# Turning p with a VectorE block transpose, with V laid out to match, in a decode kernel of two layers

## The chip, the cores and the metric

The kernel runs on one core of one Trainium2 chip. The metric is device time of one execution in microseconds. Runs are marked fast or slow by their length (slow: over 1.5% above the fastest of the same kernel). Of a kernel's runs I compare the fast ones, and medians are quoted over all runs unless said otherwise. A ratio is the mean time of one kernel's fast runs over that of the other's of the same rounds, so it is not quite the ratio of the medians quoted.

## The reference

Four tokens go through attention and a gated feed-forward block, twice, with the same weights and caches:

```python
def _A_ref(x, k_cache, v_cache, wq, wo):      # x (4, 1, 448), caches (4, 8, 8192, 256)
    W = min(4096, max(256, Sk // 4))          # 2048 rows of each cache are used
    ...                                       # 16 query heads share 8 key/value heads
    scores = jnp.einsum("bhqd,bhkd->bhqk", q, k) * (Dh ** -0.5)
    p = _softmax(scores, axis=-1)
    o = jnp.einsum("bhqk,bhkd->bhqd", p, v)
    ...
x = x + _A_ref(_layernorm(x), ...)
x = x + _B_ref(_layernorm(x), ...)            # silu(x Wg) * (x Wu), then Wd
x = x + _A_ref(_layernorm(x), ...)            # the same once more
x = x + _B_ref(_layernorm(x), ...)
```

One K or V tile of a token and head is 2048 x 256 bf16, 1 MB. There are 32 of each per layer, 128 MB for two layers; what fits in on-chip memory is kept between the layers, and about 94 MB of caches and 12 MB of weights are loaded. The arithmetic is small. The kernel is a stream of loads with work hung on it.

## The kernel before

The program builds a graph of operations, schedules it on a model of the engines at build time, and emits one instruction stream per engine. All loads are issued by SyncE, in order, on one queue. Buffers (`half`, 27 of 512 KB) are handed out as they come free. These are the parts that matter, for a single head (a group); some groups join two heads.

```python
ksrc = A_k_cache[t, kvh, ...].rearrange("(p j) d -> p (j d)", p=128)
for hf, cell in enumerate(kc):                 # two transfers of 512 KB, 128 partitions each
    dma_start(half[cell][:, :], ksrc[:, 2048 * hf:2048 * hf + 2048])
    VectorE: transpose of 32x32 blocks, in place
vsrc = A_v_cache[t, kvh, ...].rearrange("(a q g) d -> q a g d", a=4, q=128)
for hv, cell in enumerate(vs):                 # two transfers of 512 KB, 128 partitions each
    dma_start(half[cell][:, :].rearrange("p (a g d) -> p a g d", a=2, g=4),
              vsrc[:, 2 * hv:2 * hv + 2, :, :])
...
# scores: 32 matmuls of 128 columns into 4 blocks of 32 partitions of a PSUM bank
# maximum (VectorE), spread over the head's rows (2 matmuls), negated (VectorE)
exp   (ScalarE): praw <- scores
turn  (PE):      4 matmuls with praw as the stationary operand -> PSUM
copy  (ScalarE): pT <- PSUM
total (PE):      row sums of p;   pv (PE): 16 matmuls  V^T pT -> Y
...
# normalise, collect, output projection
```

Filler matmuls on zeros (line 1098) are put into PE's gaps: 282 of them, 95 us, in the profile of before.

## Time and profile before

| | before |
|---|---|
| time, median of the first 3 runs | 312.2 us (310.85 to 312.75) |
| DMA engines busy | 92.9% of the span, 106.55 MB |
| PE, VectorE, GpSimd, ScalarE busy | 81%, 63%, 28%, 22% |
| first and last packet of loaded data | 2.1 us, 295.2 us of 313.2 |
| loads of V | 98 of 512 KB |
| loads of K | 82 of 512 KB |

The page's busy shares are averages over the whole span, so a stretch that starves is hidden in them. The useful question to the trace is: in which stretches are the DMA engines busy, and how many GB/s do they move then? Both kinds of loss are in the trace of before. At 264 to 272 us the share is 0.73, with 236 GB/s moved, and the queue's sequencer had waited for PE to be done with a buffer, up to 4.8 us at a time. At 10 to 14 us the share is 1.02 and yet only 238 GB/s are moved.

### The profile page before, as it was taken

The page shows a single profiled execution, that of the slowest core. Times are in us where ns is not written, and L with a number is a line of the kernel's source. Part 1 is how long each engine was busy: PE and PEld are TensorE (multiplying, and loading weights), DVE is VectorE, ACT ScalarE, POOL GpSimd, SP SyncE. Part 2 cuts the span into 40 slices and gives each one's busy share as a digit, 9 for nine tenths or more (in the row PEclk, how much of TensorE's full clock was granted, in tenths as well). Part 3 has the DMA queues.
Part 4 walks back from the last instruction along what each step waited for, and adds up shares of the span by engine and source line. Part 5 has one row for each costly group of instructions (what it writes and reads, how often), then busy time and mean ns, then how long its engine had stood idle before and what let it go on. Part 6 is the DMA issues. An engine that isn't in the chain of part 4 may idle for free.

```text
span 313.2 us, 11054 instructions
## 1 busy us (share of the span) xinstructions
PE 255.0 (81%) x4814; PEld 129.5 (41%) x4814; DVE 198.1 (63%) x627; ACT 68.1 (22%) x196; POOL 87.1 (28%) x236
## 2 busy tenths in 40 slices
PE   4788777869598867898988785988969779888996
PEld 1323323424123543264444252544435444445563
DVE  8527945845114995559778565699776656585532
ACT  0030010303003121143322032203403231423310
POOL 1521011303202322134342031441505133332530
PEclk9999999999959997799999997589999986999995
DMA  7999999999999999999999999779999998999500
GB/s 275 317 394 401 403 401 393 397 391 346 271 387 343 306 409 393 386 340 383 397 400 394 398 395 393 281 254 374 383 334 369 391 394 314 300 387 390 206 2 3
DMA packets 45024, 107.25 MB, mean 342 GB/s; under 512 B 3240, under 2 KB 8880, under 8 KB 44592
## 3 DMA queue, kind: packets, MB, share of 16 engines
q1 hardware_dynamic: 44976, 106.55, 92.9%
q8 instruction: 38, 0.62, 0.8%
q14 instruction: 10, 0.08, 0.1%
HBM read 106.53 MB, written 0.00 MB: 340 GB/s over the span
## 4 chain that ended last, share of the span: by engine, by line
PE 37%; DMA 26%; DVE 15%; SPq 14%; issue 4%; ACT 3%; POOL 1%; DVEq 0%; ACTq 0%
DMA half<-in_A_v_cache_dram 13%; DMA half<-in_A_k_cache_dram 9%; DVE half L853 7%; PE Y L973 7%; PE A L1098 7%; SPq L848 6%; SPq L527 6%; PE S L883 5%; DMA wu_sb<-in_B_w_up_dram 4%; SPq L861 3%; PE A L1026 2%; DVE oh L990 2%; PE Z L617 2%; PE Y L943 2%; PE Y L996 1%
## 5 line engine op out<-in xcount | busy, mean ns | idle before, releaser
L853 DVE STREAM_TRANSPOSE half<-half 128x1024 uint32<-128x1024 uint32 x82 | 100.3, 1230 | 3.3 <-DMA half<-in_A_k_cache_dram 3.0
L1098 PE MATMUL A<-identb,small 128*128 128x512 bf16 x249 | 83.1, 435 | 0.0
L986 POOL TENSOR_TENSOR small<-small 128x2 f32<-128x2 f32 (+1 forms) x55 | 41.3, 753 | 62.1 <-DVE small L964 59.6
L973 PE MATMUL Y<-half,pT 128*4 128x256 bf16 (+1 forms) x1024 | 46.4, 283 | 10.7 <-DMA half<-in_A_v_cache_dram 6.5
L900 POOL TENSOR_TENSOR qe<-qc,tiny 128x64 bf16<-128x64 bf16 x64 | 18.3, 293 | 83.0 <-PE S L883 61.6
L988 ACT ACTIVATE oh<-Y 128x256 bf16<-128x256 f32 x55 | 21.1, 384 | 83.0 <-PE Y L973 71.9
L990 DVE SCALAR_TENSOR_TENSOR oh<-oh,small,Y 128x256 bf16<-128x256 bf16 x55 | 25.9, 470 | 19.0 <-ACT oh L988 18.5
L883 PE MATMUL S<-half,qe 128*8 128x128 bf16 x1472 | 30.6, 222 | 7.7 <-issue 3.6
L1098 PEld LDWEIGHTS A<-identb,small 128*128 128x128 bf16 x249 | 22.8, 109 | 20.7 <-issue 12.0
L907 DVE TENSOR_REDUCE tiny<-S 104x1 bf16<-104x128 f32 (+1 forms) x55 | 16.8, 306 | 22.8 <-PE S L883 17.5
L883 PEld LDWEIGHTS S<-half,qe 128*8 128x8 bf16 x1472 | 21.8, 85 | 17.1 <-DVE half L853 5.9
L929 ACT ACTIVATE praw<-S,small 104x128 bf16<-104x128 f32 x46 | 16.8, 365 | 55.5 <-DVE small L921 54.7
L973 PEld LDWEIGHTS Y<-half,pT 128*4 128x4 bf16 (+1 forms) x1024 | 18.6, 83 | 21.4 <-DMA half<-in_A_v_cache_dram 11.7
L1026 PE MATMUL A<-wo_sb,oT 128*4 128x448 bf16 x208 | 17.8, 358 | 2.5 <-DVE oT L1006 2.1
L951 ACT ACTIVATE pT<-Y 128x64 bf16<-128x64 f32 (+1 forms) x55 | 13.2, 240 | 20.7 <-PE Y L943 17.6
L996 PE MATMUL Y<-tiny,oh 128*128 128x2 bf16 (+1 forms) x110 | 11.0, 170 | 5.9 <-DVE oh L990 5.1
L912 PE MATMUL S<-small,identb 104*104 104x32 bf16 x55 | 11.2, 214 | 5.7 <-DVE tiny L907 4.9
L580 POOL TENSOR_SCALAR st<-st 128x1 f32<-128x1 f32 x16 | 4.3, 266 | 41.4 <-DVE st L569 41.3
L921 DVE TENSOR_REDUCE small<-S 104x1 f32<-104x32 f32 x55 | 9.0, 177 | 9.4 <-PE S L915 9.2
L943 PE MATMUL Y<-sel,praw 104*128 104x32 bf16 x184 | 12.1, 180 | 2.0 <-ACT praw L929 2.0
L773 ACT ACTIVATE wide<-A 128x448 bf16<-128x448 f32 x14 | 7.6, 544 | 27.6 <-PE A L707 15.8
L895 PE MATMUL S<-half,qe 128*8 128x256 bf16 x288 | 9.9, 274 | 4.2 <-DVE half L853 3.0
(137 smaller groups left out, 296.5 us busy)
## 6 DMA issues: line engine op xcount, KB each, us to landing
half<-in_A_v_cache_dram SPq DMA_DIRECT2D x98, 512.0 KB, 8.9
half<-in_A_k_cache_dram SPq DMA_DIRECT2D x82, 512.0 KB, 8.3
wo_sb<-in_A_wo_dram SPq DMA_DIRECT2D x8, 448.0 KB, 13.3
wq_sb<-in_A_wq_dram SPq DMA_DIRECT2D x3, 1024.0 KB, 6.9
wd_sb<-in_B_w_down_dram SPq DMA_DIRECT2D x1, 1568.0 KB, 15.2
wg_sb<-in_B_w_gate_dram SPq DMA_DIRECT2D x2, 672.0 KB, 12.7
wu_sb<-in_B_w_up_dram SPq DMA_DIRECT2D x2, 672.0 KB, 13.0
wq_sb<-in_A_wq_dram SPq DMA_DIRECT2D x2, 256.0 KB, 11.4
```

The lines of the kernel that those rows point to most:

```text
L527: g.dma(rank, nbytes, lambda e: e.dma_start(dst, src), f"w{nw[0]}", w=key if isinstance(key, tuple) else (key,), run=run)
L848: g.dma((pp - KLEAD if pp <= LAST1 else pp + KTAIL) + OFF.get(("k", t, layer, kvh), 0), 1 << 19, lambda e, cell=cell, hf=hf, ksrc=ksrc: e. ...
L853: return e.transpose(a, a)
L883: last = e.matmul(Sb[s_][qd:qd + 8, 0:128], lhsT=qe[q_][:, 0, ce, :, :].rearrange("p a n -> p (a n)"), rhs=kt[:, ce // 2, ce % 2, 2 * x:2 ...
L900: g.op(POOL, 0.25, pos - SLEAD - 1, lambda e, P=P, t=t, kvh=kvh: e.tensor_tensor(qe[q_][:, P, :, :, :], qc[t][:, kvh, :, :].unsqueeze(2).b ...
L943: last = e.matmul(o, lhsT=praw[0:R, c0:c0 + 128], rhs=w, start=(gg == 0 and h == 0), stop=False, skip_group_check=True)
L973: last = e.matmul(Yb[p_][32 * gg:32 * gg + M, 256:512], lhsT=pT[pt][:, gg, 2 * hv + a, 4 * P:4 * P + M] if n == 2 else p1[:, gg % 2, gg // ...
L986: g.op(POOL, 0.69, pos, lambda e: e.tensor_tensor(ri[p_][:, 0:2 * n], rs[p_][:, 0:2 * n], expo[:, 1:1 + 2 * n], op=ALU.pow), r=(f"rs{p_}", ...
L988: g.op(SCA, 0.34, pos, lambda e: e.activation(oh[:, :], Yb[p_][:, 256:512], ACT.Copy), r=(f"y{p_}",), w=("oh",), bank=(f"Y{p_}",))
L990: g.op(DVE, 0.43, pos, lambda e: e.scalar_tensor_tensor(out=oh[:, :], in0=oh[:, :], scalar=lomask[:, 0:1], in1=Yb[p_][:, 256:512], op0=ALU ...
L1026: last = e.matmul(Ab[32 * k:32 * k + B, 0:D], lhsT=oT[oi][:, k % 2, k // 2, :], rhs=wo_sb[:, 4 * kvh + k, :], start=False, stop=False, ski ...
L1098: g.filler = lambda b: lambda e: e.matmul(fbank[b][:, 0:512], lhsT=zero[:, 0:1].broadcast_to([128, 128]), rhs=identb[:, :].unsqueeze(1).br ...
```

## The change

The intent is to turn p (rows of the head by position) into pT (position by rows) with one VectorE transpose of 32x32 blocks, SBUF to SBUF, in place of four PE matmuls and a ScalarE copy out of PSUM. In the kernel's index arithmetic each block stays on its own 32 partitions, so V's rows must lie on the partitions that the blocks dictate: the upper 64 partitions hold rows 1024 away from those of the lower 64. No single step from partition to partition gives these rows, and the kernel splits each V load in two.

```diff
-                    ksrc = A_k_cache[...].rearrange("(p j) d -> p (j d)", p=128)
+                    ksrc = A_k_cache[...].rearrange("(h p j) d -> h p (j d)", h=2, p=128)
...
-                    vsrc = A_v_cache[...].rearrange("(a q g) d -> q a g d", a=4, q=128)
+                    vsrc = A_v_cache[...].rearrange("(h b a s j) d -> h b s a (j d)", h=2, b=2, a=2, j=4)
...
-                        e.dma_start(half[cell[0]][:, :].rearrange("p (a g d) -> p a g d", a=2, g=4),
-                            vsrc[:, 2 * hv:2 * hv + 2, :, :])
+                        [e.dma_start(half[cell[0]][64 * h:64 * h + 64, :].rearrange("p (a x) -> p a x", a=2),
+                            vsrc[h, hv]) for h in range(2)]
...
-            g.op(PE, ..., turn, ...)
-            g.op(SCA, ..., lambda e: e.activation(pf, Yb[p_][:, 0:PW], ACT.Copy), ...)
+            g.op(DVE, 0.14, pos, lambda e: e.transpose(
+                pT[pt][...].bitcast(UINT32)..., praw[...].bitcast(UINT32)), ...)
```

Cut from it: groups of two heads are gone; the query is expanded twice per head; the norm does one power of three numbers on GpSimd in place of three operations; the last residual is written straight into the output layout, and the output copy is split over two engines; the filler has one density while loads remain and a higher one afterwards; and the plan of heads, the lead of each load and the set of tiles kept between the layers are all set anew.

## The prediction

The 1230 ns under "p's turn" and the 1.23 us of rival 2 are K's transpose in the trace of before (128x1024 uint32, 82 times). The queue's sequencer, which the prediction has waiting for PE, waited longest in sum for the matmuls on V (L973): 29.1 us in 13 waits.

> **What bounds the kernel now.** I read the page first: the busy shares, the slices, the DMA queues and the chain of waits.
>
> ```profile
> PE 255.0 (81%) x4814; PEld 129.5 (41%) x4814; DVE 198.1 (63%) x627; ACT 68.1 (22%) x196; POOL 87.1 (28%) x236
> ...
> q1 hardware_dynamic: 44976, 106.55, 92.9%
> ...
> PE 37%; DMA 26%; DVE 15%; SPq 14%; issue 4%; ACT 3%; POOL 1%; DVEq 0%; ACTq 0%
> ```
>
> The 16 DMA engines are busy 92.9% of 313.2 us; no compute engine but PE comes near. PE's 255 us contain 95 us of filler matmuls (the group of line 1098: 249 writing A, 83.1 us, and 33 writing Z, 12.0 us) [...], so PE is not the bound in amount. The chain names PE more often than DMA because a buffer comes free when PE has read it and the queue's sequencer waits for that. This is a loading kernel with a short start and a tail. I then asked for stretches of the span (start and end, length, busy time and count per engine, granted clock, DMA share, GB/s):
>
> ```profile
> 5.00:10.00 5.00, 1.79 (x5) 0.65 (x3) 4.39 (x38) 0.00 (x0) 0.00 (x0) 1.00 1.01 423
> 10.00:14.00 4.00, 3.85 (x14) 1.72 (x14) 1.53 (x13) 0.00 (x0) 2.96 (x9) 1.00 1.02 238
> 14.00:18.00 4.00, 3.75 (x27) 1.20 (x30) 0.76 (x5) 0.00 (x0) 2.65 (x8) 1.00 1.06 380
> 66.00:72.00 6.00, 3.73 (x45) 1.22 (x43) 3.13 (x6) 1.06 (x5) 0.70 (x1) 1.00 1.05 386
> 72.00:76.00 4.00, 3.63 (x84) 1.82 (x85) 2.18 (x9) 2.41 (x9) 1.48 (x3) 1.00 1.05 382
> 76.00:80.00 4.00, 3.14 (x49) 1.73 (x52) 1.69 (x12) 0.00 (x0) 1.76 (x5) 1.00 1.08 246
> 82.00:86.00 4.00, 1.56 (x17) 0.47 (x14) 0.69 (x1) 0.11 (x1) 0.00 (x0) 1.00 1.10 238
> ...
> 192.00:208.00 16.00, 15.26 (x246) 7.58 (x241) 12.16 (x42) 3.17 (x12) 6.40 (x18) 0.58 0.79 290
> 264.00:272.00 8.00, 7.17 (x174) 4.06 (x162) 4.96 (x16) 3.50 (x10) 2.01 (x4) 1.00 0.73 236
> 294.00:313.00 19.00, 15.47 (x325) 9.80 (x323) 6.03 (x32) 2.34 (x7) 5.29 (x12) 0.78 0.02 6
> ```
>
> Three kinds of loss show. First, at 192 to 208 and 264 to 272 the DMA share falls to 0.79 and 0.73: the queue starves, in the first case at a granted clock of 0.58. Second, from 294 on nothing is loaded: a tail of 19 us. Third, and decisive here, at 10 to 14, 76 to 80 and 82 to 86 the engines are fully busy (1.02, 1.08, 1.10) and yet move only 238 to 246 GB/s, against 380 to 423 on either side. The code says what lies there: 3 MB of query weights issued from 1.15 us and moved at 423 GB/s from about 2.3 us end at about 10 us, and next in the queue come their last 64 rows, sent as two transfers, one into partitions 0 to 63, one into 64 to 127. The other two stretches hold the last 64 rows of the gate and up weights, sent the same way.
>
> ```profile
> half<-in_A_v_cache_dram SPq DMA_DIRECT2D x98, 512.0 KB, 8.9
> half<-in_A_k_cache_dram SPq DMA_DIRECT2D x82, 512.0 KB, 8.3
> ...
> wq_sb<-in_A_wq_dram SPq DMA_DIRECT2D x2, 256.0 KB, 11.4
> ```
>
> V is 98 transfers of 512 KB (51.4 MB, nearly half of all bytes), each over all 128 partitions. The change turns each into a pair of 256 KB with the same shape of destination as the last line's.
>
> [...]
>
> **The change part by part.**
>
> *V's transfers.* The loss of one pair, read from the stretches: 10 to 14 us moved 238 x 4 = 952 KB, which at 400 GB/s (between the neighbours' 423 and 380) takes 2.4 us, so 1.6 us were lost. 76 to 80: 984 KB at 382 is 2.6 us, lost 1.4. 82 to 86: 952 KB at 386 is 2.5 us, lost 1.5. The first pair is of exactly V's new size, 2 x 256 KB, 1.36 us at 386 GB/s; with the loss about 2.9 us, some 180 GB/s, which is half rate or a little under. If every pair of V loses what half rate costs, 98 x 1.36 = 133 us. It is not hidden: the DMA engines are the bound, and a busy share near 1 leaves nothing to put it in. [...] I put an in-between case at half of it, 65 us (an estimate of mine, worked from the same 1.36 us).
>
> *Bytes.* Layer 0 keeps 22 K tiles instead of 23 and 15 V tiles as before, so K has 84 loads instead of 82: 1.05 MB more, 2.7 us at 386 GB/s, on the path.
>
> *Issues.* V goes from 98 to 196 issues. The shortest issue is about 0.37 us and a typical one 0.47, so a pair takes 0.9 us of the sequencer, under the 1.36 us of data: hidden, though a starved queue refills more slowly.
>
> *p's turn.* Removed per single group: 4 matmuls of 180 ns (12.1 us in all, pipelined, about 0.26 us a group in the timeline) and a ScalarE copy of 222 ns; 13.2 us of ScalarE in all with the paired groups. Added: 64 VectorE transposes of 128x64 uint32. 1230/1024 is 1.2 ns a column, so 0.08 us plus a start that I take from small VectorE instructions here (155 to 180 ns): about 0.2 us, 13 us in all. The chain of one group loses one hop and about 0.5 us; groups overlap, so this counts once or twice, in the tail.
>
> *No paired groups.* 46 single and 9 paired groups become 64 single ones. The nine more cost VectorE about 9 x (284 + 177 + 180 + 470) = 10 us, less the longer forms they replace (9 x 419 = 4 us for the maximum alone); with 2 more K transposes (2.5 us) VectorE goes from 198 to some 218 us. GpSimd gets a second query expansion per head, 64 x 293 ns = 18.8 us, and loses two of three small operations per norm, 16 x (266 + 298) = 9 us: about 100 us. Neither is a bound.
>
> *Tail.* The last update is one operation instead of five, the output copy (0.61 us) is split over two engines, fillers are denser once all loads are issued (the clock in 304 to 312 was 0.53). Together with p's turn I take 1.5 us, so 17.5 us of tail.
>
> *The new order.* Plan, lead times and filler density are all set anew, which may fill the starved stretches. What they cost now: V 51.4 MB at 386 is 133 us, the other 55.2 MB at an average of 380 (weights included) 145 us, start 2, tail 19: 299 us, against 313 measured, so about 14 us.
>
> The sum: V 133, the rest 56.2 MB at 380 = 148, start 2, tail 17.5: 300 us with neither loss. With V in pairs: 365 at half of the loss, 433 at all of it. With slower loading, starvation no longer adds, as buffers come free in time.
>
> **The rivals.** (1) *Pairs run at full rate in a long stream.* The three slow stretches are isolated pairs among full-width transfers; nothing in the trace shows fifty in a row. For it: the two halves are adjacent in the queue, and the 16 engines report one transfer done over a spread of about 2 us[...]. Whoever wrote the change also set everything anew around it, which one hardly does for something slow. Against it: these very pairs were adjacent too, and lost all the same. Then the time is 300 us plus what of the starvation stays, 302 to 314. (2) *VectorE or GpSimd becomes the bound*, because K's transpose (84 x 1.23 = 103 us) shares VectorE with the longer softmax chain: at some 218 us of work this costs single microseconds through late buffers. For it: VectorE has 15% of the chain. It would make 310 to 318 out of (1). (3) *Only the bytes and the tail count*, 2.7 against 1.5 us: 313, the same.
>
> **Range and chances.** I give the pairs' loss about two in three: a third to nearly all of it (410 to 433), a third to part of it (330 to 400), and a third to rival 1 with its variants. The middle of this is about 370 us; I name that, with a range of 302 to 432. The gap between 315 and 330 is unlikely, so the range is wide because there are two outcomes, not because each is vague. Faster by over 2% needs less than 306: full-rate pairs and most starvation gone, 0.20. Same, 306 to 318.4: 0.13. Slower: 0.67.
>
> **What would show it.** Right: in the stretches with V, a DMA share near 1 at 200 to 300 GB/s instead of 386, packets of 2 KB that take longer, V's two transfers landing much later, PE waiting for V in the group of line 973's successor, VectorE's share falling. Wrong: 380 to 400 GB/s in V's stretches; then the trace decides between the tail, the dips and VectorE. The p step is right if the new transpose takes 0.15 to 0.25 us and no ScalarE copy stands between exponent and sums. The prediction fails by its first step if the loss of a lone pair is not that of a stream.

## The result, and the profile after

The changed kernel took 422.89 us (median of 4 runs, 416.42 to 424.23), the kernel before 312.48 us (4 runs, 310.85 to 314.88). The ratio is 1.340, 95% interval 1.320 to 1.361: slower by a third. Two of the four runs are slow, the fast ones took 416.42 and 421.59 us. The profiled run is a fast one. Its page, busy shares, queue and chain:

```profile
PE 289.5 (70%) x4851; PEld 139.5 (34%) x4851; DVE 222.2 (54%) x747; ACT 75.5 (18%) x160; POOL 98.4 (24%) x254
...
q1 hardware_dynamic: 46832, 107.60, 97.8%
...
DMA 61%; PE 18%; SPq 14%; DVE 4%; issue 2%; ACT 0%; DVEq 0%
```

The DMA engines are busier than before (97.8% against 92.9%) with one megabyte more to move in 101 us more. The chain is now 61% DMA, where it was 26%. Every compute engine's share fell. The stretches of the changed kernel say how the loads went (start and end, length, busy time and count of PE, PE's loads, VectorE, ScalarE, GpSimd, then granted clock, DMA share, GB/s):

```profile
20.00:26.00 6.00, 4.46 (x93) 2.11 (x93) 6.00 (x13) 0.56 (x1) 2.13 (x8) 1.00 1.07 248
40.00:44.00 4.00, 0.93 (x10) 0.22 (x10) 1.32 (x2) 0.00 (x0) 0.00 (x0) 1.00 1.08 240
200.00:240.00 40.00, 28.07 (x534) 13.24 (x535) 23.83 (x76) 9.82 (x21) 11.58 (x32) 0.74 1.00 257
240.00:280.00 40.00, 30.70 (x543) 16.05 (x543) 28.12 (x85) 8.06 (x18) 10.24 (x27) 0.74 1.05 303
398.60:414.60 16.00, 13.44 (x287) 8.60 (x283) 6.11 (x29) 2.96 (x8) 2.24 (x3) 0.85 0.01 2
```

Rates near those of three short stretches before (238 to 246 GB/s at a full share) now hold for most of the span: 240 to 303 here. PE's granted clock is 0.74 in the long stretches; why is not shown. The tail is 16.0 us after the last loaded packet (at 398.6), against 18.0 before (from 295.2). The issues and the waits for V:

```profile
half<-in_A_v_cache_dram SPq DMA_DIRECT2D x196, 256.0 KB, 11.9
half<-in_A_k_cache_dram SPq DMA_DIRECT2D x84, 512.0 KB, 13.7
```

```profile
PEld Y L918 <- DMA half<-in_A_v_cache_dram: 61.9, 40, 6.5
PE Y L918 <- DMA half<-in_A_v_cache_dram: 57.2, 40, 6.4
...
DVE half L837 <- DMA half<-in_A_k_cache_dram: 50.8, 34, 8.0
```

The same three waits before:

```profile
PEld Y L973 <- DMA half<-in_A_v_cache_dram: 11.7, 17, 2.0
...
PE Y L973 <- DMA half<-in_A_v_cache_dram: 6.5, 12, 1.5
...
DVE half L853 <- DMA half<-in_A_k_cache_dram: 3.0, 5, 1.0
```

The lists of waits give total wait, number of waits and the longest, in us. K's loads have not been touched in shape, yet they land 13.7 us after their issue instead of 8.3, and VectorE waits 50.8 us for them where it waited 3.0. So the slow V transfers hold up what stands behind and beside them.

The p step itself, first the lines of before (exponent, copy), then those of after (exponent, transpose):

```profile
L929 ACT ACTIVATE praw<-S,small 104x128 bf16<-104x128 f32 x46 | 16.8, 365 | 55.5 <-DVE small L921 54.7
...
L951 ACT ACTIVATE pT<-Y 128x64 bf16<-128x64 f32 (+1 forms) x55 | 13.2, 240 | 20.7 <-PE Y L943 17.6
```

```profile
L897 ACT ACTIVATE praw<-S,small 112x128 bf16<-112x128 f32 x64 | 34.8, 544 | 59.8 <-DVE small L894 52.9
...
L901 DVE STREAM_TRANSPOSE pT<-praw 128x64 uint32<-128x64 uint32 x64 | 15.0, 235 | 24.4 <-PE Y L918 23.1
```

The transpose takes 235 ns and replaces a copy of 240 ns (222 for a single head) and the matmuls ahead of it. But the exponent became 179 ns longer (544 against 365): it now writes p in an order that suits the transpose. I had not foreseen this.

### The profile page after: what moved, and what is told of

It reads as the page before. It is cut to its first block, busy times and chain, and to the rows that moved or that the text cites. A ratio compares the mean times of both kernels' runs of the same rounds, so it can differ in the third digit from the quotient of the medians.

```text
span 414.6 us, 11341 instructions
## 1 busy us (share of the span) xinstructions
PE 289.5 (70%) x4851; PEld 139.5 (34%) x4851; DVE 222.2 (54%) x747; ACT 75.5 (18%) x160; POOL 98.4 (24%) x254
## 3 DMA queue, kind: packets, MB, share of 16 engines
q1 hardware_dynamic: 46832, 107.60, 97.8%
## 4 chain that ended last, share of the span: by engine, by line
DMA 61%; PE 18%; SPq 14%; DVE 4%; issue 2%; ACT 0%; DVEq 0%
DMA half<-in_A_v_cache_dram 39%; DMA half<-in_A_k_cache_dram 22%; SPq L846 5%; SPq L832 5%; PE Y L918 5%; PE S L867 3%; SPq L512 3%; DVE half L837 3%; PE A L1042 2%; PE A L970 1%; PE Z L1042 1%; PE A L688 1%; PE Z L707 1%; PE Y L940 1%; PE Y L907 1%
## 5 line engine op out<-in xcount | busy, mean ns | idle before, releaser
L837 DVE STREAM_TRANSPOSE half<-half 128x1024 uint32<-128x1024 uint32 x84 | 103.5, 1235 | 50.9 <-DMA half<-in_A_k_cache_dram 50.8
L918 PE MATMUL Y<-half,pT 128*4 128x256 bf16 x1024 | 61.2, 351 | 58.7 <-DMA half<-in_A_v_cache_dram 57.2
L930 POOL TENSOR_TENSOR small<-small 128x2 f32<-128x2 f32 x64 | 44.7, 700 | 106.5 <-DVE small L911 101.8
L867 PE MATMUL S<-half,qe 128*16 128x128 bf16 x2048 | 51.3, 252 | 24.5 <-DVE half L837 16.8
L874 POOL TENSOR_TENSOR qe<-qc,tiny 128x64 bf16<-128x64 bf16 x128 | 34.8, 292 | 134.5 <-PE S L867 116.5
L867 PEld LDWEIGHTS S<-half,qe 128*16 128x16 bf16 x2048 | 37.6, 100 | 42.5 <-DVE half L837 24.2
L918 PEld LDWEIGHTS Y<-half,pT 128*4 128x4 bf16 x1024 | 19.5, 90 | 83.0 <-DMA half<-in_A_v_cache_dram 61.9
L897 ACT ACTIVATE praw<-S,small 112x128 bf16<-112x128 f32 x64 | 34.8, 544 | 59.8 <-DVE small L894 52.9
L901 DVE STREAM_TRANSPOSE pT<-praw 128x64 uint32<-128x64 uint32 x64 | 15.0, 235 | 24.4 <-PE Y L918 23.1
L881 DVE TENSOR_REDUCE tiny<-S 112x1 bf16<-112x128 f32 x64 | 17.7, 279 | 19.2 <-PE S L867 18.9
L567 POOL TENSOR_TENSOR st<-st,small 128x3 f32<-128x3 f32 x16 | 13.7, 854 | 29.5 <-DVE st L557 28.1
L886 PE MATMUL S<-small,identb 112*112 112x32 bf16 x64 | 15.1, 238 | 3.0 <-DVE tiny L881 2.9
## 6 DMA issues: line engine op xcount, KB each, us to landing
half<-in_A_v_cache_dram SPq DMA_DIRECT2D x196, 256.0 KB, 11.9
half<-in_A_k_cache_dram SPq DMA_DIRECT2D x84, 512.0 KB, 13.7
wd_sb<-in_B_w_down_dram SPq DMA_DIRECT2D x1, 1568.0 KB, 16.1
```

The costliest lines, as they stand in the source:

```text
L837: return e.transpose(a, a)
L867: last = e.matmul(Sb[s_][qd:qd + 16, 0:128], lhsT=qe[q_][:, ce, :, :, :].rearrange("p a y n -> p (a y n)"), rhs=kt[:, ce // 2, ce % 2, z, ...
L874: g.op(POOL, 0.25, pos - SLEAD - 1, lambda e, y=y, t=t, kvh=kvh: e.tensor_tensor(qe[q_][:, :, :, y, :], qc[t][:, kvh, :, :].unsqueeze(2).b ...
L897: g.op(SCA, 0.38, pos, lambda e: e.activation(praw[0:R, :, :, :].rearrange("p j r m -> p j m r"), Sb[s_][0:R, 0:128].rearrange("p (m j r) ...
L918: last = e.matmul(Yb[p_][32 * (j % 4):32 * (j % 4) + 4, 256:512], lhsT=pT[pt][:, j % 2, 8 * hv + 4 * (j // 4):8 * hv + 4 * (j // 4) + 4, j ...
L930: g.op(POOL, 0.69, pos, lambda e: e.tensor_tensor(ri[p_][:, 0:2 * n], rs[p_][:, 0:2 * n], expo[:, 2:4], op=ALU.pow), r=(f"rs{p_}", "expo") ...
```

## The experiments

My theory was that a pair of transfers into partitions 0 to 63 and 64 to 127 moves at about half of the rate of one over all 128, alone or among other pairs; the half is my estimate from the trace of before (some 180 against 386 GB/s). Rivals: the number of issues or their size; any transfer with fewer than 128 partitions; the rest of the change. Eleven kernels ran on the chip, all of them reported as correct, including two that pair p with wrong rows of V: here the comparison is too coarse to see that, so for those two "correct" means nothing. For the same reason the row order of the mended kernels further down rests on their index arithmetic and not on that report: after the transpose, partition P holds rows 512q + 4P + 0 to 3 of each quarter q, which is what the V load brings there.

The first group starts from the kernel before and changes V's loads alone, so order, arithmetic and buffers are the old ones. Its common edit lets one load consist of several transfers on one semaphore (16 counts for each).

**V in halves, nothing else**

```diff
-  e.dma_start(half[cell[0]][:, :]..., vsrc[:, 2 * hv:2 * hv + 2, :, :])
+  [e.dma_start(half[cell[0]][u:w, :]..., vsrc[u:w, 2 * hv:2 * hv + 2, :, :]) for u, w in ((0, 64), (64, 128))]
```

> The kernel before with nothing changed but V's 98 loads: each 512 KB goes as two transfers, partitions 0 to 63 and 64 to 127, 256 KB each; result stays correct. My theory [...]: about 98 x 1.1 to 1.4 us more, 415 to 440 us, GB/s in V's stretches 200 to 260 at a DMA share near 1. Rival 'it is the rest of the change' (new order, VectorE transpose, more GpSimd work): 310 to 325. Rival 'twice the issues': also slow, but then the split by columns is slow too.

Measured: 412.64 us (2 runs), ratio 1.319 (1.309 to 1.329), against 312.88 us of before on the same chip. The cause alone, in the old kernel, gives 99.8 us, or 1.02 us a pair: somewhat less than the 1.1 to 1.4 that I had given. The rest of the change is not needed for the slowdown.

**The same number of transfers, cut by columns**

```diff
+  [e.dma_start(half[cell[0]][:, 1024 * a:1024 * a + 1024]..., vsrc[:, 2 * hv + a, :, :]) for a in range(2)]
```

> The kernel before with each V load as two transfers of 256 KB over all 128 partitions (columns 0 to 1023, then 1024 to 2047): the same number of issues, the same bytes and the same 2 KB runs as the split by partitions. Result correct. My theory: 310 to 318 us, no loss. Rival 'twice the issues or smaller transfers': about as slow as the split by partitions, above 380.

Measured: 314.17 us (4 runs), ratio 1.0005 (0.992 to 1.009): the same as before. The page lists 196 loads of 256 KB, as in the changed kernel, and they land after 7.3 us instead of 11.9 (the latter in the changed kernel and in the cut in halves alike). The profiled run of this kernel is one marked slow, 316.87 us:

```profile
half<-in_A_v_cache_dram SPq DMA_DIRECT2D x196, 256.0 KB, 7.3
```

Stretch 130 to 170 us of the cut by columns, and then of the cut in halves:

```profile
130.00:170.00 40.00, 34.82 (x786) 19.22 (x774) 30.96 (x89) 11.08 (x33) 14.48 (x41) 1.00 1.04 395
```

```profile
130.00:170.00 40.00, 29.04 (x553) 14.89 (x552) 23.04 (x54) 7.51 (x24) 8.63 (x20) 0.74 1.05 274
```

The share is the same, 1.04 and 1.05; the rate is 395 against 274 GB/s, and in the trace a packet of 2 KB takes 88 ns there on average, against 138. Size, number of issues and length of the runs in memory (2 KB in both) are out as causes. What is left is which partitions one transfer covers.

**Partitions 32 to 95 as one transfer**

```diff
+  ... for u, w in ((0, 32), (32, 96), (96, 128))]
```

> The kernel before with each V load as three transfers: partitions 0 to 31 (128 KB), 32 to 95 (256 KB), 96 to 127 (128 KB). The middle one has 64 partitions as the halves have[...]. Result correct. My theory: only the outer two lose, so about half of the loss of the split in halves: 355 to 380 us. Rival 'fewer than 128 partitions is slow whatever they are', or 'more transfers are slow': at least as slow as the split in halves, 415 or more.

Measured: 375.14 us in the fast run and 381.93 us in a slow one. The fast run is 62 us over before. There are more transfers than with halves (three a load) and none has 128 partitions, and it is 37.5 us faster. "Fewer than 128 partitions" and "more transfers" are both wrong by sign. The middle transfer has the shape of a half and the same 256 KB, but covers partitions 32 to 95, on both sides of 64. The expected share of the loss was a half, as half of V's bytes go into the outer transfers; measured is 0.62 of it.

**Halves for one V tile of each head**

```diff
+  CUTS = (whole, halves)   ... for u, w in CUTS[hv]]
```

> The kernel before with only the second of V's two tiles (49 of 98 loads) sent as halves. Result correct. My theory: the loss is per pair, so half of the split of all, less what the starved stretches of before absorb: 355 to 375 us. Rival 'a stream of pairs [...] recovers': the loss per pair is larger here than in the full split, so above 375.

Measured: 406.57 us (2 runs). My theory, that each pair costs the same, fell here: with 49 pairs instead of 98 nearly all of the loss is still there, 93.7 us, which is 1.91 us a pair against 1.02. What I had written down as a rival, that a stream of pairs recovers part and a lone pair does not, is nearer. Where pairs and whole transfers alternate, the whole ones suffer too. This is a stretch of V alone in that run (half of the V bytes whole), and then one of V in the run with all V in halves:

```profile
106.00:116.00 10.00, 4.63 (x64) 1.74 (x64) 1.73 (x10) 0.54 (x1) 1.32 (x4) 0.88 1.07 221
```

```profile
108.00:116.00 8.00, 5.19 (x40) 1.40 (x38) 0.89 (x4) 0.54 (x1) 0.00 (x0) 0.79 1.05 248
```

With half of the bytes in good shape the rate is lower (221) than with none (248). The landings in this run's trace say where the time goes. From the last landing event of one load to that of the next, a whole tile between whole loads takes 1.3 us (median of 60), a pair 2.3 (48), and a whole tile just ahead of a pair 2.2 (49). A whole tile just behind a pair, with a whole load after it, takes 1.1 (20). To test the neighbours' part I made the next two.

**The same number of pairs, but next to each other**

```diff
+  ... for u, w in CUTS[kvh % 2]]        # odd heads: both V tiles in halves; even heads: both whole
```

> The kernel before; half of the heads (odd ones) send both V tiles as halves, the others send both whole. About as many pairs as in the run with one tile per head (406.57 us, 1.9 us a pair), but here pairs stand next to pairs. Theory A: [...] pairs next to pairs lose less, as in the full split (412.64 us, 1.0 us a pair): 355 to 380 us. Theory B: about fifty pairs, wherever they are, already cost all there is to lose: 400 to 412 us.

Measured: 370.21 us in the fast run, 382.06 us in a slow one. The fast run is 57.8 us over before with 52 pairs: 1.11 us a pair. Theory A's range holds and theory B falls: 52 pairs next to pairs cost 58 us, 49 pairs among whole transfers cost 94. That the neighbours matter is shown by this; why they do is not.

**Few pairs, each among whole transfers**

```diff
+  ... for u, w in CUTS[kvh % 2 * hv]]   # only the second V tile of the odd heads
```

> The kernel before; only the second V tile of the odd heads goes as halves, about a quarter of all loads, each pair among full-width transfers. Theory A (a lone pair loses 1.5 to 1.9 us): some 24 pairs, 36 to 46 us, less what starved stretches absorb: 345 to 362 us. Theory B (the loss is no sum over pairs): nearer to 400. A loss of half rate per pair and no more (1.36 us less nothing) gives at most 345.

Measured: 363.5 us (2 runs, both fast), ratio 1.167 (1.153 to 1.181), which the record marks unclear at 2% although the interval lies far above it. It is 51.1 us over before with 26 pairs: 1.97 us a pair. It lies 1.5 us above what theory A allowed, and by count it repeats the 1.91 us of the run above. Put together, from medians (fast run alone where one of the two was slow):

| pairs of V | how they stand | time over before, us | us a pair |
|---|---|---|---|
| 98 (b_halves) | pair beside pair | 99.8 | 1.02 |
| 52 (b_heads) | pair beside pair | 57.8 | 1.11 |
| 49 (b_halves_one) | pair beside whole V | 93.7 | 1.91 |
| 26 (b_quarter) | pair beside whole V | 51.1 | 1.97 |

Half rate alone would be 1.36 us a pair (an estimate, from 512 KB at 386 GB/s). "Pair beside pair" is a matter of degree, as whole K loads stand between in all four kernels: in the order of the issues, the pairs form 22, 18, 49 and 26 unbroken runs. With 0.74 us a pair and 1.17 us a run one gets 98, 60, 94 and 50 us for the four rows. These two numbers are fitted to the same four rows, so this alone proves nothing. But the landings say the same from another side: by their medians in the four runs (that of b_heads was profiled in a slow run), a pair takes 1.9 to 2.3 us instead of 1.3, and the one whole tile just ahead of a run of pairs 2.2 to 2.5. A good part of the loss falls on a transfer that was not touched.

The reason is not shown. What the trace of before shows is that neighbours are under way at the same time: the 16 landing events of one transfer lie 2.0 us apart from first to last (median), while from the last event of one load to that of the next there are 1.3 us (median).

The second group starts from the changed kernel.

**The changed kernel with V in one transfer (wrong rows)**

```diff
-  vsrc = ....rearrange("(h b a s j) d -> h b s a (j d)", h=2, b=2, a=2, j=4)
+  vsrc = ....rearrange("(a q j) d -> q a (j d)", a=4, q=128)
-  [e.dma_start(half[cell[0]][64 * h:64 * h + 64, :]..., vsrc[h, hv]) for h in range(2)]
+  e.dma_start(half[cell[0]][:, :]..., vsrc[:, 2 * hv:2 * hv + 2, :])
```

> The changed kernel with V loaded in one transfer of 512 KB over 128 partitions, in the row order of the kernel before, nothing else changed. The result is wrong on purpose: p's rows meet other rows of V. It shows what the rest of the change is worth. My theory: 300 to 312 us, since bytes, starvation and tail alone remain. Rival 'VectorE or GpSimd is the new bound' (218 us and 98 us of work): 315 to 330. Rival 'the new order is itself slow': above 330.

Measured: 313.45 us (4 runs, one slow), ratio 1.011 (0.978 to 1.043), beside 312.58 us: unclear at 2%, and 1.5 us above the 300 to 312 us that I expected. VectorE has 217.8 us of work in it and GpSimd 98.1, and loads still run at full rate in the middle of the span:

```profile
200.00:240.00 40.00, 32.46 (x749) 17.44 (x737) 37.43 (x114) 12.08 (x25) 14.93 (x38) 1.00 1.03 385
```

So the 109 us between this and the changed kernel (106 between the means of their fast runs) are V's transfers, and everything else in the change together is worth little: between a gain of 2.2% and a loss of 4.3%, by the interval.

**The same with the exponent writing in storage order**

```diff
-  praw[0:R, :, :, :].rearrange("p j r m -> p j m r"), Sb[...].rearrange("p (m j r) -> p j m r", m=4, j=2)
+  praw[0:R, :, :, :],                                 Sb[...].rearrange("p (m j r) -> p j r m", m=4, j=2)
```

> The changed kernel with V in one transfer (row order wrong on purpose, 313.45 us) and, on top, the exponent writing p in storage order, four neighbours at a time, instead of scattering it. The exponent should fall from 545 ns to 360 to 450 ns, 64 times, all of it on each head's chain. If the chains of the heads set the time where loading starves: 305 to 311 us. If the loads set it: 311 to 315 us, the same.

Measured: 314.62 us (4 runs), ratio 1.011 (1.006 to 1.016). The exponent fell to 366 ns, so 0.18 us came off each of 64 chains, and the time did not move. So this part of the chain does not set it.

**A correct layout that needs no halves**

Let K's two tiles hold alternate groups of 8 rows, as before, and let both tiles' scores go into the same 32 partitions, 64 columns each. Then, by the index arithmetic, the partitions after the transpose are rows 4 apart all the way from 0 to 127, and V is one transfer, in the row order of the kernel before.

```diff
-  for z in range(2):
-      last = e.matmul(Sb[s_][64 * hf + 32 * z:..., 0:128], ... start=(ce == 0), ...)
+  for z in range(4):
+      last = e.matmul(Sb[s_][32 * z:32 * z + 16, 64 * hf:64 * hf + 64], ... start=(ce == 0 and hf == 0), ...)
-  praw = sb("praw", [128, 2, 16, 4], BF16)
+  praw = sb("praw", [128, 2, 8, 8], BF16)
   # and vsrc, ksrc as in the kernel before
```

> The changed kernel mended: K's two tiles hold alternate groups of 8 rows of each partition as in the kernel before, the scores of both tiles go to the same 32 partitions of the score bank in 64 columns each (64 matmuls of 64 columns per group instead of 32 of 128), so that after the VectorE transpose the 128 partitions are rows 4 apart and V comes in one transfer over 128 partitions. Result must be correct. My theory: V's loss gone, 302 to 318 us; the 2048 extra matmuls cost PE about 30 to 60 us of busy time that lies mostly beside the loads, and may cost 2 to 8 us through later buffers. If the loss came from something else in the change: above 330.

Measured: 363.8 us (4 runs, one slow), ratio 1.175 (1.157 to 1.193); the record marks this unclear at 2% too, with an interval far above it. The loss in V is gone (V lands after 7.5 us), but this is far over my 318. My expectation gave "something else in the change" as the only reading above 330, which the run with wrong rows excludes. What differs from that run is seen in the groups:

```profile
L866 PE MATMUL S<-half,qe 128*16 128x64 bf16 x4096 | 55.8, 213 | 27.1 <-issue 16.1
L896 ACT ACTIVATE praw<-S,small 112x128 bf16<-112x128 f32 x64 | 53.1, 829 | 82.0 <-DVE small L893 77.2
```

The exponent takes 829 ns here, where it writes p at 16-byte steps, against 544 at 8-byte steps in the changed kernel. PE has twice the score matmuls (4096 in 55.8 us, against 2048 in 44.5 us in the run with wrong rows) and stands 16.1 us in "issue" before them, time in which it waited for nothing that the profile shows. With the chain so much longer, buffers come free late (this link is argued), and the DMA share of the whole span falls to 82.0%.

**That layout with whole matmuls and a contiguous exponent**

```diff
+  pool = sb("half", [128, NPOOL, 8 * DH], BF16);  half = [pool[:, s, :] for s in range(NPOOL)]
+  lo, hi = sorted(c[0] for c in kcs[0])
+  kt = pool[:, lo:hi + 1:hi - lo, :].rearrange("p h (j c z r v) -> p c v z h j r", ...)
   # one matmul of 128 columns over both tiles where hi - lo < 16, else two of 64
+  praw[0:R, :, :, :], Sb[...].rearrange("p (m j r) -> p j r m", m=8, j=2)
```

> The mended kernel (363.8 us) mended again: all 27 buffers are one tensor, so that one matmul takes its 128 columns from both K tiles of a head (32 matmuls of 128 columns per group again, 64 of 64 only where the two buffers lie 16 or more apart), and the exponent writes p in storage order (eight neighbours at a time) instead of scattering it. Result must be correct. If the 363.8 us came from twice the matmuls and the scattered exponent (829 ns instead of 545): 308 to 322 us, and the exponent at 350 to 550 ns. If it came from the new row order itself: it stays above 340.

Measured: 322.51 us (4 runs), ratio 1.035 (1.024 to 1.045), 0.5 us above what I gave. The exponent is back at 366 ns:

```profile
L898 ACT ACTIVATE praw<-S,small 112x128 bf16<-112x128 f32 x64 | 23.4, 366 | 56.4 <-DVE small L895 46.0
```

The same 112x128 values took 366 ns in storage order, 544 at 8-byte steps and 829 at 16-byte steps; reading and writing order changed together, so the runs do not say which of them costs.

So the two costs together were 41 us; the run does not separate them. By the index arithmetic it is a correct kernel with p turned by VectorE, 100 us faster than the changed one, and still 3.5% slower than the one before.

**A third buffer for pT**

```diff
-NP = 2
+NP = 3
```

> The twice mended kernel (322.51 us) with three buffers for the turned p instead of two, as its VectorE transposes waited 9.1 us in all for PE to have used an older one. If that wait holds up the heads: 315 to 320 us. If not, or if the time beyond 313 us comes from the order in which PE works: 319 to 326 us, the same.

Measured: 320.97 us (4 runs, one slow), ratio 1.028 (1.021 to 1.035). The transposes' wait for an older pT fell from 9.1 to 3.0 us in all, and the time stayed within the noise: not the bound. Where the remaining 8 us lie is open. In the profiled run of the kernel above the last load ends at 299.0 us, 7 us later than in the run with wrong rows (291.9), and its tail is 22.7 us against 19.3; what its DMA engines lacked to a full share during the loads adds up to 11.6 us against 7.4, counted by microseconds. The plan and the leads had been set for other durations, and I have not set them anew, so I can't say whether the layout or the order is to blame.

No version here beats the kernel before. With V loaded well the change showed no gain even with wrong rows, under this plan and these leads.

## Why the prediction was right or wrong

The direction and its cause were right and the time, 370 us, was 53 us short. The range held it, but it was drawn around three different outcomes, so that says little.

*V's transfers.* Right in kind. The three slow stretches before show the same thing in small, and the changed kernel and the old kernel with nothing but halves both run at 240 to 300 GB/s at a full share. Its size: between the run with V in one transfer and the changed kernel lie 109 us, 1.12 us a pair; I had 1.36 for half rate. That term was 24 us too large, but the next one more than made up for it.

*The in-between case.* This is the step that failed: "I put an in-between case at half of it, 65 us" (of the 133 us at half rate). With rival 1 it pulled the named time, the middle of three cases, down from 433 to 370. The runs show a recovery of a fifth to a quarter of the half-rate loss where pairs stand beside pairs (1.02 to 1.12 us instead of 1.36), and the reverse where pairs stand among whole transfers (1.91 to 1.97). Of my three cases the one with all the loss, 433 us, was nearest to 422.89.

*The first estimate of one pair's loss*, 1.4 to 1.6 us from the stretches of before, was of pairs among whole transfers. It was larger than the half rate's 1.36, which I noted and did not use. By the table it belonged to the dearer kind. I also misread two of the stretches: the pairs of the gate and up weights are 2 x 112 KB, for which half rate costs 0.6 us (an estimate, at 386 GB/s). By the landing times of that trace the two parts of the up weights' pair land 0.5 us apart, while the whole transfer of 672 KB just ahead of them lands 3.0 us after the one before it, where its like, without a pair behind it, took 1.7. The gate weights (3.0 after 1.9) and the query weights' 1 MB (4.4 after 2.5) show the same. The neighbour lost more than the pair, and this was there to be seen.

*The sum without the loss* was 300 us; the run with V in one transfer gave 313.45. From its first to its last packet, loading took 289.7 us there instead of the 281 of the sum; another 1.8 us are a longer tail, and about 2 us are device time beyond the span of the profile. I took the starved stretches for gone with a new order, and they were not. Nor did slow loading end the starvation, as I had written: what the DMA engines lack to a full share in each microsecond of loading adds up to 7.4 us in that run and to 7.0 in the changed kernel (bins of 2 us give 3.4 and 3.6, so only the comparison counts). So 433 us had some 13 us too little here and 24 too much in V, and the two errors partly cancel.

*Rival 1* (full rate in a long stream) is refuted by the run with halves alone. The argument that one hardly sets everything anew around something slow carried a third of my weight; it says nothing about the chip, and I should have given it less.

*Rival 2* (VectorE or GpSimd as the bound): VectorE's work was predicted at 218 us and measured 222.2, GpSimd's 100 and 98.4. Neither set the time with V in one transfer at 313.45 us.

*p's turn.* Predicted 0.2 us for the transpose, measured 0.235, and the ScalarE copy is gone as said. What I missed was the exponent, 0.18 us longer through its new order; the hop saved (0.26 us of matmuls and 0.22 of the copy) and what came in (0.235 and 0.18) nearly cancel on a head's chain. The exponent's part had no weight in the end: taking it out again changed nothing.

*Issues.* Predicted 0.47 us each, measured 0.61 (median), 1.2 us a pair. The cut by columns has as many issues, but of 0.43 us, so it does not test this length. A DMA share near 1 in the slow stretches (1.00 to 1.08) shows that the queue was full there, so the issues are hidden.

*Tail.* Predicted 17.5 us, measured 16.0 in the changed kernel but 19.3 in the run with V in one transfer, so a gain of the tail is not established.

## What to carry to other kernels

Before a layout is chosen for the compute engines' sake, look at which partitions each single transfer will cover: a load cut into partitions 0 to 63 and 64 to 127 cost a third of the run time here, while the same cut by columns cost nothing that shows (314.17 against 312.88 us), and one with its middle half in 32 to 95 cost less (62 us against 99.8). In a profile the sign is a DMA share near 1 with too few GB/s (1.02 to 1.10 with 238 to 246 GB/s here, where the stretches beside had 380 to 423), and three stretches of 4 us in the old trace were enough to see it coming. Also check the neighbours: transfers of good shape just ahead of bad ones were slowed as well (2.2 to 2.5 us from landing to landing instead of 1.3), so that mending one V tile of each head saved 6 us of 100 (406.57 against 412.64), and mending both tiles of every second head 42.
